# Layer two's input products taken in pairs of tiles, their low tail products on 64 rows each

## The chip, the core and the metric

One core of one Trainium2 chip runs the whole program. The time is device microseconds (us) of one execution. Engines are named as in the profile: PE (TensorE matmul), PEld (its weight loads), DVE (VectorE), ACT (ScalarE), POOL (GpSimd) and SP (SyncE, which issues the DMAs).

## What is computed

A softmax over seven weights per head and token makes a causal convolution of x, then two feed-forward layers follow, the first with a rational activation, the second with a clipped one. Everything is float32 in the reference.

```python
w = exp(weight_gen - max); w = w / (sum(w) + 1e-9)          # 7 weights per head
x = einsum("bshk,bskhg->bshg", w, unfolded_x)               # 8192 tokens x 192
h = x @ w_in                                                # 192 -> 2048
g = (a0 + a1*h + a2*h**2 + a3*h**3) / (1 + |b0|*|h| + |b1|*h**2 + 1e-6)
x = g @ w_out                                               # 2048 -> 192
h = x @ w_in2                                               # 192 -> 2048
out = (h * clip(h + 3, 0, 6) / 6) @ w_out2                  # 2048 -> 192
```

## The kernel before

The 8192 tokens go in 17 batches: two of 256 tokens and fifteen of 512. The 2048 inner features are 16 tiles of 128. A slice is one PSUM bank of 512 columns: one tile of a 512-token batch, or two tiles of a 256-token batch. That makes 256 slices for each layer.

Products of float32 accuracy are made of reduced-precision ones (float32r): each operand is cut into a high part and the low rest. The 192 input rows are a head of 128 and a tail of 64. For one tile, `mm_in` (L254) issues five products into the tile's bank: high weight by high x, high weight by low x and low weight by high x for the head; and for the tail two products with `wst`, whose upper 64 rows hold the high and whose lower 64 rows the low tail weights, while x's tail stands twice, in rows 0 to 63 and again in 64 to 127. So the first tail product gives high and low weights by high x together, and the second does the same with low x. `in1` (L282) calls `mm_in` for layer one, `in2` (L383) for layer two. `out1` (L362) makes five products of 512 columns for a tile of layer one's output, `out2` (L403) 32 products of 192 columns and full float32 for a quarter of layer two's output of 256 tokens.

Between `in1` and `out1` ACT, DVE and POOL make the rational function: seven operations on ACT, DVE and POOL's three (`pool_q`, `pool_m`, `pool_lo`, L308 to L357) among them. After `in2` come one Relu on ACT (`act_r2`, L388) and one operation on DVE (`dve_g2`, L395), which frees the bank. The convolution's multiplications (`conv_mul`, L158) run on POOL too, eight for a 512-token batch.

PSUM has six banks for this work: at most four slices of layer one (class h), and at most four of all else (class s: `in2`, transposes, `out2`, weight decoding). Weights come as pairs of 32-bit words and are decoded and cut by ACT, DVE and POOL in the first 150 us ("jobs": `in`, `pair` for the tail weights, `o1`, `o2`).

The order of all instructions is made before the program is written: `plan` (L746) is a list scheduler. It takes operations with a cost, a due time (in units of T) and their dependences, and appends to each engine what can start first, weighed by due time. Each engine then runs its list strictly in that order. The numbers NB to EV (L560 to L586) set due times and weights; the costs are written at `add`. They are the planner's figures, not times of the chip.

Of the kernel before, what the change touches and what calls it, by code (L numbers as in the profile page):

```python
# [19 lines left out]
def kernel(  # L20
# [230 lines left out]
            op=ALU.subtract,  # L251
        )

    def mm_in(i, xs, f, dst):  # L254
        xh, xl = xs
        w = win[i]
        fs = slice(f * P, (f + 1) * P)
        seq = [
            (w["hi"], xh[:, 0, :]),
            (w["hi"], xl[:, 0, :]),  # L260
            (w["lo"], xh[:, 0, :]),
            (wst[i], xh[:, 1, :]),
            (wst[i], xl[:, 1, :]),
        ]
        for n, (l, r) in enumerate(seq):
            nc.tensor.matmul(  # L266
                out=dst, lhsT=l[:, fs], rhs=r, start=(n == 0), stop=(n == len(seq) - 1),
                skip_group_check=True,
            )

    h1 = {}
    e1 = {}
# [108 lines left out]
    h2 = {}  # L381

    def in2(b, q):  # L383
        h = h2[b, q] = bank(("in2", b, q), [P, GW], "h2")
        for i in range(BF[b]):
            mm_in(1, xin[1, b], q * BF[b] + i, cols(b, h, i))
# [113 lines left out]
    def job_pair(i, c):  # L500
        src = (moe_w_in, moe2_w_in)[i]
        ss = [slice(k * CW * WS, (k + 1) * CW * WS) for k in (c, c + 1)]
        top, low = (wst[i][h * 64 : (h + 1) * 64, c * CW : (c + 2) * CW] for h in range(2))

        def cuts(w):
            a, z = w[0:64], w[64:P]
            return [
                cut(top[:, :CW], low[:, :CW], a),
                cut(low[:, CW:], low[:, CW:], z),
                (lambda: nc.scalar.activation(out=top[:, CW:], in_=z, func=AF.Copy), None),  # L510
            ]

        return dict(shape=[P, CW], src=[src[P:D, ss[0]], src[P:D, ss[1]]], cuts=cuts)
# [44 lines left out]
                    l(eng)  # L558

    NB = {"u": 2, "w": 3, "l": 2, "r0": 3, "ghi": 3, "glo": 2}  # L560
    T = 4.407
    X0P = -112.0
    LP = -8.378
    JP0 = 4.004
    JPT = 3.728
    JPU = 1.292
    PEN = 1.749
    CP = 5.419
    KP = 0.04
    WIN = 26.752  # L570
    SWL = 0.0
    BETA = 0.009
    C1 = -5.774
    CV = 5.626
    SM = 4.098
    XQ = -4.798
    XTP = 4.081
    XH = 2.095
    O1 = 4.281
    UM = 5.526  # L580
    I2 = -0.923
    SPR = 0.935
    R2 = 2.049
    O2 = 4.361
    OS = 0.653
    EV = 3.556  # L586
    ops = {}

    def op(key, eng, cost, prio, emit, after=(), take=(), lat=None):
# [41 lines left out]
    for u, (b, v) in enumerate(UB):  # L631
        t0 = S0[b] * T - (BV[b] - 1 - v) * 8 * T
        c = u // 2
        if u % 2 == 0:
            t = t0 - CV * T
            add("gen", "SP", 0.6, t - XQ * T if c else X0P, load_gen, c, lat=2.0,
                take=[("wg", 2, [("softmax_b", c)])])
            add("load", "SP", 5.3, t - XQ * T + 1.0 if c else X0P + 0.5, load_chunk, c, lat=2.0,
                take=[("x", 2, [("conv_mul", 2 * c + 1, 1, 1)])])
            add("softmax_a", "DVE", 1.7, t - SM * T, softmax_a, c, after=[("gen", c)])  # L640
            add("softmax_e", "ACT", 0.28, t - SM * T + 2.0, softmax_e, c, after=[("softmax_a", c)])
            add("softmax_b", "DVE", 2.7, t - SM * T + 4.0, softmax_b, c, after=[("softmax_e", c)],
                take=[("wk", 2, [("conv_mul", 2 * c + 1, 1, 1)])])
        for i in range(2):
            for z in range(2):
                t = t0 - CV * T + (2 * i + z) * T
                prev = [(u, i, 0)] if z else [(u, 0, 1)] if i else []
                flex = (("POOL", 1.25, 0.0), ("DVE", 0.85, CP))[: 1 + (u < 2)]
                add("conv_mul", flex, 0, t, lambda u, i, z, e="POOL": conv_mul(u, i, z, e), u, i, z,
                    after=[("load", c), ("softmax_b", c)] + [("conv_mul",) + k for k in prev],  # L650
                    take=[("prod", 2, [("conv_sum", u, i, z)])])
                add("conv_sum", "DVE", 0.78, t + 0.5 * T, conv_sum, u, i, z,
                    after=[("conv_mul", u, i, z)] + [("conv_sum",) + k for k in prev],
                    take=[("xc", 2, [("xT", u)])] if i + z == 0 else [])
        add("x_dup", "ACT", 0.2, t0 - XTP * T, x_dup, u, after=[("conv_sum", u, 1, 1)])
        add("xT", "PE", 0.44, t0 - XTP * T + 0.5, xT, u, after=[("x_dup", u)], lat=0.2,
            take=[("s", NS, [("x_lo", u)])])
        add("x_hi", "ACT", 0.5, t0 - XTP * T + 1.0 - XH, x_hi, u, after=[("xT", u)],
            take=[("xh0", 2, [("in1", S0[b] + SN[b] - 1)])] if v == 0 else [])
        add("x_lo", "DVE", 0.6, t0 - XTP * T + 1.6 - XH, x_lo, u, after=[("x_hi", u)])  # L660
    for b in range(len(BL)):
        n, last = BT[b], S0[b] + SN[b] - 1
        ca, cd = 0.066 + n / 1200, 0.075 + n / 960
        t = (last + O1 + 2) * T
        add("mid_y", "ACT", 0.22 + 2 * ca, t - UM * T, mid_y, b,
            after=[("out1", last)], take=[("ys", 1, [("mid_f", b)])])
        add("mid_f", "DVE", cd, t + 0.1 - UM * T, mid_f, b, after=[("mid_y", b)])
        add("mid_head", "ACT", ca, t + 0.2 - UM * T, mid_head, b, after=[("mid_y", b)],
            take=[("xh1", 1, [("in2", b, SN[b] - 1)])])
        add("mid_tail", "ACT", ca, t + 0.3 - UM * T, mid_tail, b,  # L670
            after=[("mid_f", b), ("mid_head", b)])
        add("head_lo", "DVE", cd, t + 0.4 - UM * T, head_lo, b, after=[("mid_head", b)])
        add("tail_lo", "DVE", cd, t + 0.5 - UM * T, tail_lo, b,
            after=[("mid_tail", b), ("head_lo", b)])
        cm = 5 * BF[b] * (0.0137 + n / 2400)
        tu = t + I2 * T
        for q in range(SN[b]):
            t2 = tu + q * T * SPR * BF[b] / 2
            f = (q + 1) * BF[b] - 1
            jobs_in = [done["in", 1, f // 4], done["pair", 1, f // 8 * 2]]  # L680
            add("in2", "PE", cm, t2, in2, b, q, lat=0.2,
                after=[("tail_lo", b), ("head_lo", b)] + jobs_in
                + ([("in2", b, q - 1)] if q else []),
                take=[("s", NS, [("dve_g2", b, q)])])
            add("act_r2", "ACT", 0.48, t2 + 1.0 - R2 * T, act_r2, b, q,
                after=[("in2", b, q)] + ([("act_r2", b, q - 1)] if q % 2 else []),
                take=[] if q % 2 else [("big", ST, [("out2", b, BV[b] - 1, (f + BF[b]) * 4 // NF)])])
# [58 lines left out]
    def plan():  # L746
# [26 lines left out]
        while len(seq) < len(ops):  # L773
            best = None
            banks = opens()
            any_open = min(banks)[0]
            class_open = {}
            for name, most in LIMIT.items():
                mine = sorted((t for t, n in banks if n == name), reverse=True)
                class_open[name] = max(any_open, mine[most - 1] if len(mine) >= most else 0.0)  # L780
            for e, rs in ready.items():
                pick = None
                while todo[e] and todo[e][-1]["key"] in end:
# [1 line left out]
                cur = todo[e][-1]["prio"] if todo[e] else 0.0  # L785
                for at, o, cost, pen in rs:
                    at = max(at, free[e])
                    for name, depth, _ in o["take"]:
                        if name in LIMIT:
                            at = max(at, class_open[name])  # L790
                            continue
                        ring = rings.get(name, [])
                        if len(ring) >= depth:
# [16 lines left out]
                run = run + cost if o["key"][0] in FULL else 0.0  # L810
            free[e] = at + cost
            end[o["key"]] = at + cost + (LAT[e] if o["lat"] is None else o["lat"])
            for name, depth, rel in o["take"]:
                if name in LIMIT:
                    i = min(range(NSB), key=lambda i: (banks[i][0], i))
                    slot[o["key"]] = i
                    held[i] = (name, rel)
                    continue
                rings.setdefault(name, []).append(rel)
# [42 lines left out]
```

## Time and profile before

| | us |
|---|---|
| median of three runs | 1333.9 (1333.36 to 1335.59) |
| the profiled execution, its own time | 1331.12 |
| its span, first to last instruction | 1329.3 |
| PE busy in the span | 1254.5 |
| POOL busy | 1174.8 |
| ACT busy | 1154.4 |
| DVE busy | 1104.0 |

The profiled execution lies 2.8 us under the median, and 1.8 us of it lie outside the span. The mean granted TensorE clock is 0.976 of full speed. A record of a matmul lasts longer than the distance to the next one, since matmuls overlap; what one costs in a dense row is the distance from start to start.

### The profile page before, as it was taken

The page shows a single profiled execution, that of the slowest core. Times are in us where ns is not written, and L with a number is a line of the kernel's source. Part 1 is how long each engine was busy: PE and PEld are TensorE (multiplying, and loading weights), DVE is VectorE, ACT ScalarE, POOL GpSimd, SP SyncE. Part 2 cuts the span into 40 slices and gives each one's busy share as a digit, 9 for nine tenths or more (in the row PEclk, how much of TensorE's full clock was granted, in tenths as well). Part 3 has the DMA queues.
Part 4 walks back from the last instruction along what each step waited for, and adds up shares of the span by engine and source line. Part 5 has one row for each costly group of instructions (what it writes and reads, how often), then busy time and mean ns, then how long its engine had stood idle before and what let it go on. Part 6 is the DMA issues. An engine that isn't in the chain of part 4 may idle for free.

```text
span 1329.3 us, 18514 instructions
## 1 busy us (share of the span) xinstructions
PE 1254.5 (94%) x6256; PEld 1097.1 (83%) x6256; DVE 1104.0 (83%) x1649; ACT 1154.4 (87%) x2064; POOL 1174.8 (88%) x934
## 2 busy tenths in 40 slices
PE   2567998999999999999999999999999999999998
PEld 2566996888988889898888989888888988888898
DVE  6888988989789897989789897898978898886841
ACT  5989998989899898989989898988989899898941
POOL 7999999999989999899988999889998999987830
PEclk9577998999999999999999999999999999999999
DMA  7323000100010100101010000100000000000000
GB/s 221 118 80 97 23 18 6 34 16 31 7 36 7 43 1 13 34 10 36 6 37 4 16 31 7 36 14 31 7 29 14 7 6 7 7 1 12 1 13 12
DMA packets 16119, 37.62 MB, mean 28 GB/s; under 512 B 1948, under 2 KB 12314, under 8 KB 16024
## 3 DMA queue, kind: packets, MB, share of 16 engines
q1 hardware_dynamic: 16024, 36.44, 8.5%
q8 instruction: 49, 0.80, 0.2%
q14 instruction: 46, 0.38, 0.1%
HBM read 30.14 MB, written 6.29 MB: 27 GB/s over the span
## 4 chain that ended last, share of the span: by engine, by line
PE 47%; ACT 21%; POOL 16%; DVE 9%; issue 6%; DMA 1%; SPq 0%; POOLq 0%; DVEq 0%; ACTq 0%
PE h L266 24%; PE y L410 12%; POOL w L346 5%; POOL w L309 5%; POOL glo L357 3%; ACT r L324 3%; ACT w L295 3%; ACT r L329 3%; ACT w L333 3%; ACT u L290 2%; ACT g L393 2%; PE y L374 2%; PE y L376 2%; PE y L378 2%; PE y L377 2%
## 5 line engine op out<-in xcount | busy, mean ns | idle before, releaser
L357 POOL TENSOR_TENSOR glo<-w,r 128x512 fp32r<-128x512 f32 x256 | 332.3, 1299 | 37.0 <-DVE w L350 19.5
L346 POOL TENSOR_TENSOR w<-w,ghi 128x512 f32<-128x512 f32 x256 | 331.9, 1299 | 27.8 <-DVE ghi L338 16.9
L309 POOL TENSOR_TENSOR w<-w,u 128x512 f32<-128x512 f32 x256 | 333.3, 1303 | 22.2 <-ACT w L295 13.4
L410 PE MATMUL y<-wo,g 128*128 128x192 f32 x2048 | 351.6, 326 | 0.0
L410 PEld LDWEIGHTS y<-wo,g 128*128 128x128 f32 x2048 | 338.3, 190 | 8.8
L295 ACT ACTIVATE w<-u,bab 128x512 f32<-128x512 f32 x256 | 209.8, 819 | 25.5 <-POOL glo L357 24.9
L338 DVE SCALAR_TENSOR_TENSOR ghi<-h,acol,r 128x512 fp32r<-128x512 f32 x256 | 190.6, 745 | 34.6 <-ACT r L329 29.2
L350 DVE SCALAR_TENSOR_TENSOR w<-h,acol,w 128x512 f32<-128x512 f32 x256 | 191.0, 746 | 32.6 <-POOL w L346 31.0
L266 PE MATMUL h<-xh,wst 128*128 128x512 f32 (+1 forms) x544 | 209.3, 385 | 1.8 <-POOL wst L488 1.8
L397 DVE SCALAR_TENSOR_TENSOR g<-g,h 128x512 f32<-128x512 f32 x256 | 174.7, 682 | 42.7 <-ACT g L393 41.9
L266 PE MATMUL h<-xl,wst 128*128 128x512 f32 (+1 forms) x544 | 208.9, 384 | 0.0
L302 ACT ACTIVATE l<-h,acol 128x512 f32<-128x512 f32 x256 | 200.7, 784 | 3.9 <-PE h L266 2.4
L313 DVE TENSOR_TENSOR l<-h,l 128x512 f32<-128x512 f32 x256 | 174.2, 685 | 35.7 <-ACT l L302 33.4
L324 ACT ACTIVATE r<-w 128x512 f32<-128x512 f32 x256 | 161.9, 632 | 44.3 <-POOL w L309 43.4
L164 POOL TENSOR_TENSOR prod<-x,wk 128x672 f32<-128x672 f32 x127 | 189.4, 1510 | 11.7 <-DMA x<-in_x_dram 4.5
L317 DVE SCALAR_TENSOR_TENSOR h<-l,acol,h 128x512 f32<-128x512 f32 x256 | 191.5, 751 | 7.4 <-ACT u L290 3.4
L393 ACT ACTIVATE g<-h 128x512 f32<-128x512 f32 x256 | 153.6, 600 | 18.2 <-PE h L266 17.9
L329 ACT ACTIVATE r<-r 128x512 f32<-128x512 f32 x256 | 161.2, 630 | 2.0
L290 ACT ACTIVATE u<-h 128x512 f32<-128x512 f32 x256 | 152.1, 594 | 9.9 <-PE h L266 9.7
L333 ACT ACTIVATE w<-w 128x512 f32<-128x512 f32 x256 | 160.2, 626 | 0.0
L266 PE MATMUL h<-xh,win0hi 128*128 128x512 f32 (+1 forms) x272 | 115.6, 425 | 15.8 <-DVE w L350 14.5
L266 PEld LDWEIGHTS h<-xh,wst 128*128 128x128 f32 x544 | 106.1, 195 | 21.6 <-POOL wst L488 2.1
(74 smaller groups left out, 2235.9 us busy)
## 6 DMA issues: line engine op xcount, KB each, us to landing
x<-in_x_dram SPq DMA_DIRECT2D x14, 960.0 KB, 4.6
st<-in_moe_w_out_dram SPq DMA_DIRECT2D x16, 384.0 KB, 3.2
out_dram<-osb SPq DMA_DIRECT2D x32, 192.0 KB, 1.9
st<-in_moe_w_in_dram SPq DMA_DIRECT2D x8, 512.0 KB, 5.8
st<-in_moe_w_in_dram SPq DMA_DIRECT2D x8, 256.0 KB, 6.1
wg<-in_weight_gen_dram SPq DMA_DIRECT2D x16, 112.0 KB, 2.0
x<-in_x_dram SPq DMA_DIRECT2D x1, 768.0 KB, 10.3
x<-in_x_dram SPq DMA_DIRECT2D x2, 216.0 KB, 4.6
```

The lines of the kernel that those rows point to most:

```text
L266: nc.tensor.matmul(out=dst, lhsT=l[:, fs], rhs=r, start=(n == 0), stop=(n == len(seq) - 1), skip_group_check=True,)
L295: nc.scalar.activation(out=w, in_=e1[sl]["u"], func=AF.Identity, scale=bab[:, 1:2], bias=bab[:, 0:1])
L302: nc.scalar.activation(out=l, in_=h1[sl], func=AF.Identity, scale=acol[:, 3:4], bias=acol[:, 2:3])
L309: nc.gpsimd.tensor_tensor(out=e["w"], in0=e["w"], in1=e["u"], op=ALU.mult)
L317: nc.vector.scalar_tensor_tensor(out=h, in0=e["l"], scalar=acol[:, 1:2], in1=h, op0=ALU.add, op1=ALU.mult)
L324: nc.scalar.activation(out=r, in_=e["w"], func=AF.Ln, bias=CEPS)
L329: nc.scalar.activation(out=r, in_=r, func=AF.Exp, scale=-1.0)
L333: nc.scalar.activation(out=w, in_=w, func=AF.Copy, bias=CEPS)
L346: nc.gpsimd.tensor_tensor(out=m, in0=m, in1=g1[sl][0].bitcast(F32), op=ALU.mult)
L350: nc.vector.scalar_tensor_tensor(out=m, in0=h1.pop(sl), scalar=acol[:, 0:1], in1=m, op0=ALU.add, op1=ALU.subtract)
L357: nc.gpsimd.tensor_tensor(out=glo, in0=e["m"], in1=e["r"], op=ALU.mult)
L410: nc.tensor.matmul(out=y2[b, v][:, s, :], lhsT=g2[b, q][:, c : c + P], rhs=wo2[:, n, :], start=(n == 0 and s == 0), stop=(n == NF - 1), sk ...
```

## The change

For the fifteen batches of 512 tokens, `in2` now handles two tiles at a time, q and q + 1. It takes two PSUM banks, issues the first four products of tile q and the first four of tile q + 1, and then one low tail product for each. The low tail product is no longer made on all 128 rows: `mm_low` multiplies 64 rows of `wst` by 64 rows of low x, rows 0 to 63 for an even tile and rows 64 to 127 for an odd one. The product of low weight and low x is dropped by this. So that an odd tile finds its high tail weights in the lower half, the two halves of layer two's `wst` are exchanged for odd tiles: `job_pair` now cuts them with four copies on ACT where there were three, and four subtractions on 64 x 256 elements where there were two on 64 x 512.

The planner counts the pair as one PE operation of 2.2 (before: two of 1.135), lets it take two banks at once, and has new numbers T to EV; the cost of `conv_mul` on POOL is 1.36 where it was 1.25. `SWL` is 14.0 where it was 0.0, which gives other work on PE a small penalty while a row of `out2` operations is shorter than 14 us.

```diff
+    def mm_low(i, xs, f, dst):
+        rows = slice(f % 2 * 64, f % 2 * 64 + 64)
+        nc.tensor.matmul(
+            out=dst, lhsT=wst[i][rows, f * P : (f + 1) * P], rhs=xs[1][rows, 1, :],
+            start=False, stop=True, skip_group_check=True,
+        )
...
-        for n, (l, r) in enumerate(seq):
+        for n, (l, r) in enumerate(seq[: 4 if half else 5]):
...
     def in2(b, q):
+        if BF[b] == 1:
+            for n in (q, q + 1):
+                h2[b, n] = bank(("in2", b, n), [P, GW], "h2")
+                mm_in(1, xin[1, b], n, h2[b, n], True)
+            for n in (q, q + 1):
+                mm_low(1, xin[1, b], n, h2[b, n])
+            return
...
+                (ha, da), (hz, dz) = cut(ta, None, a), cut(lz, None, z)
+                return [
+                    (ha, cut(ta[e], la[e], a[e])[1]),
+                    (hz, cut(lz[o], tz[o], z[o])[1]),
+                    (cut(la[o], None, a[o])[0], cut(ta[o], ta[o], a[o])[1]),
+                    (cut(tz[e], None, z[e])[0], cut(lz[e], lz[e], z[e])[1]),
+                ]
...
-    T = 4.407
+    T = 4.526
...
-    SWL = 0.0
+    SWL = 14.0
...
-                flex = (("POOL", 1.25, 0.0), ("DVE", 0.85, CP))[: 1 + (u < 2)]
+                flex = (("POOL", 1.36, 0.0), ("DVE", 0.85, CP))[: 1 + (u < 2)]
...
-        cm = 5 * BF[b] * (0.0137 + n / 2400)
+        two_f = BF[b] == 1
+        cm = 2.2 if two_f else 5 * BF[b] * (0.0137 + n / 2400)
...
+                    take=[("s", NS, [("dve_g2", b, k)], ("in2", b, k)) for k in qs])
```

On PE, in the middle of the program, before: one tile of layer two (`win1` and `wst_82` are layer two's weights, `xh` and `xl` the high and low x, `h` the bank) and behind it one of layer one (`win0`, `wst_81`).

```order
L266 MATMUL h_6800<-xh_6647,win1hi 128x512 [waits DVE_49]
L266 MATMUL h_6800<-xl_6648,win1hi 128x512
L266 MATMUL h_6800<-xh_6647,win1lo 128x512
L266 MATMUL h_6800<-xh_6647,wst_82 128x512
L266 MATMUL h_6800<-xl_6648,wst_82 128x512
L266 MATMUL h_6812<-xh_5953,win0hi 128x512 [waits DVE_49]
L266 MATMUL h_6812<-xl_5954,win0hi 128x512
L266 MATMUL h_6812<-xh_5953,win0lo 128x512
L266 MATMUL h_6812<-xh_5953,wst_81 128x512
L266 MATMUL h_6812<-xl_5954,wst_81 128x512
```

The same place on PE now, one pair of layer two's tiles:

```order
L266 MATMUL h_6805<-xh_6659,win1hi 128x512 [waits Activation_49]
L266 MATMUL h_6805<-xl_6660,win1hi 128x512
L266 MATMUL h_6805<-xh_6659,win1lo 128x512
L266 MATMUL h_6805<-xh_6659,wst_82 128x512
L266 MATMUL h_6810<-xh_6659,win1hi 128x512 [waits DVE_49]
L266 MATMUL h_6810<-xl_6660,win1hi 128x512
L266 MATMUL h_6810<-xh_6659,win1lo 128x512
L266 MATMUL h_6810<-xh_6659,wst_82 128x512
L273 MATMUL h_6805<-xl_6660,wst_82 128x512
L273 MATMUL h_6810<-xl_6660,wst_82 128x512
```

The number of matmuls is the same; the low tail product of the first tile moved behind the second tile's four products, the wait for the second bank stands in the middle of the pair, and the two rows of L273 are the products on 64 rows each.

On ACT, in the same part of the program, before: the two Relus (`g2<-h2`) that fill one pair of results, with operations of layer one (`l`, `u`) between them.

```order
L393 ACTIVATE g2_6213<-h2_6193 128x512
L302 ACTIVATE l_6217<-h1_6159,acol_74 128x512
L290 ACTIVATE u_6226<-h1_6207 128x512
L302 ACTIVATE l_6230<-h1_6207,acol_74 128x512
L393 ACTIVATE g2_6213<-h2_6219 128x512
```

Now:

```order
L407 ACTIVATE g2_6288<-h2_6257 128x512
L407 ACTIVATE g2_6288<-h2_6262 128x512
L297 ACTIVATE u_6299<-h1_6282 128x512
L309 ACTIVATE l_6302<-h1_6282,acol_74 128x512
L302 ACTIVATE w_6318<-u_6299,bab_76 128x512
```

Both Relus of a pair stand behind each other, since both banks are finished together.

On SP, at the start of the program, before: the loads of weights (`st`), of the convolution's weights (`wg`) and of x, in the order in which they are issued.

```order
L431 DMA st<-in_moe_w_in_dram 64x1024 x2
L431 DMA st<-in_moe_w_in_dram 128x1024 x3
L431 DMA st<-in_moe_w_in_dram 64x1024 x2
L431 DMA st<-in_moe_w_out_dram 128x2x384
L97 DMA wg<-in_weight_gen_dram 128x224
L118 DMA x<-in_x_dram 128x1536
```

Now:

```order
L445 DMA st<-in_moe_w_in_dram 64x1024 x2
L445 DMA st<-in_moe_w_in_dram 128x1024 x3
L97 DMA wg<-in_weight_gen_dram 128x224
L118 DMA x<-in_x_dram 128x1536
```

The second block of x moved ahead of the second pair of tail weights and the first output weights.

## Rows read from the trace of the kernel before

**Rows 1.** Page, part 1: busy us (share of the span) x instructions.

```profile
PE 1254.5 (94%) x6256; PEld 1097.1 (83%) x6256; DVE 1104.0 (83%) x1649; ACT 1154.4 (87%) x2064; POOL 1174.8 (88%) x934
```

**Rows 2.** Windows: length, busy us of each engine (x instructions), granted clock, DMA.

```profile
0.00:150.00 150.00, 90.33 (x500) 81.43 (x501) 126.28 (x198) 127.19 (x243) 132.59 (x117) 0.81 0.37 115
150.00:300.00 150.00, 144.95 (x727) 125.50 (x727) 132.85 (x204) 137.10 (x247) 143.59 (x114) 0.98 0.07 22
300.00:700.00 400.00, 397.00 (x1945) 344.74 (x1944) 346.88 (x516) 361.07 (x643) 375.87 (x296) 1.00 0.06 22
700.00:1300.00 600.00, 596.33 (x2940) 520.75 (x2939) 493.83 (x728) 525.00 (x929) 522.70 (x411) 1.00 0.04 13
1300.00:1330.00 30.00, 25.87 (x151) 24.71 (x149) 4.12 (x6) 4.01 (x8) 0.00 (x0) 1.00 0.04 14
```

**Rows 3.** Waits of PE, 150 to 1250 us: us in total, times, longest.

```profile
PE y L374 <- DVE xl L249: 9.4, 4, 4.6
PE y L377 <- POOL glo L357: 1.2, 1, 1.2
```

**Rows 4.** Chain in order of time: start us, us, what; three starts of layer two, one `out2` quarter.

```profile
990.05 3.41 PE h L266 x15
...
1041.10 2.60 PE y L410 x16
...
1066.33 3.45 PE h L266 x15
...
1142.62 3.42 PE h L266 x15
```

**Rows 5.** Timeline of PE, 699 to 712 us: start us, us, instruction.

```profile
700.75 0.39 PE L266 MATMUL h<-xh,win1hi 128*128 128x512 f32 x1
700.98 0.39 PE L266 MATMUL h<-xl,win1hi 128*128 128x512 f32 x1
...
711.85 0.39 PE L378 MATMUL y<-glo,wo1s 128*128 128x512 f32 x1
```

**Rows 6.** Timeline of PE around one `out2` quarter.

```profile
731.38 2.76 PE L410 MATMUL y<-wo,g 128*128 128x192 f32 x16
733.85 0.53 PE L266 MATMUL h<-xh,win0hi 128*128 128x512 f32 x1
734.21 0.40 PE L266 MATMUL h<-xl,win0hi 128*128 128x512 f32 x1
```

**Rows 7.** Timeline of POOL, 400 to 420 us.

```profile
413.97 1.48 POOL L164 TENSOR_TENSOR prod<-x,wk 128x672 f32<-128x672 f32 x1 [1.13 <-DVE wk L139]
415.30 1.28 POOL L346 TENSOR_TENSOR w<-w,ghi 128x512 f32<-128x512 f32 x1
416.55 1.27 POOL L309 TENSOR_TENSOR w<-w,u 128x512 f32<-128x512 f32 x1
```

**Rows 8.** Groups by line: busy us, mean ns of one, idle before.

```profile
L397 DVE SCALAR_TENSOR_TENSOR g<-g,h 128x512 f32<-128x512 f32 x256 | 174.7, 682 | 42.7 <-ACT g L393 41.9
L393 ACT ACTIVATE g<-h 128x512 f32<-128x512 f32 x256 | 153.6, 600 | 18.2 <-PE h L266 17.9
```

**Rows 9.** Groups by line and form: the cuts of weights on POOL.

```profile
L488 POOL TENSOR_TENSOR wst<-st,wst 64x512 fp32r<-64x512 f32 x8 | 10.4, 1305 | 0.6
L488 POOL TENSOR_TENSOR wo1l<-st,wo1h 128x256 fp32r<-128x256 f32 x7 | 5.3, 758 | 0.0
```

**Rows 10.** Chain in order of time, the first 50 us.

```profile
6.60 6.93 DMA st<-in_moe_w_in_dram
13.55 7.95 DMA x<-in_x_dram
...
44.57 1.32 POOL wst L488
48.17 2.47 PE h L266 x10
```

More of the change, by code (lines that the diff above doesn't have):

```diff
@@ L252, in tail_lo, with mm_in @@
         )
-    def mm_in(i, xs, f, dst):
+    def mm_in(i, xs, f, dst, half=False):
         xh, xl = xs
@@ L506, in cuts @@
             a, z = w[0:64], w[64:P]
+            if i == 1:
+                ta, la, tz, lz, a, z = (
+                    x.rearrange("p (f two c) -> p f two c", two=2, c=P)
+                    for x in (top[:, :CW], low[:, :CW], top[:, CW:], low[:, CW:], a, z)
+                )
+                e, o = (slice(None), slice(None), 0), (slice(None), slice(None), 1)
+                (ha, da), (hz, dz) = cut(ta, None, a), cut(lz, None, z)
[5 more added lines that the diff above has]
+                ]
             return [
@@ L560 @@
     NB = {"u": 2, "w": 3, "l": 2, "r0": 3, "ghi": 3, "glo": 2}
-    T = 4.407
+    T = 4.526
     X0P = -112.0
[L563 to L568, printed above, removed]
+    LP = -24.816
+    JP0 = 7.655
+    JPT = 3.582
+    JPU = 2.557
+    PEN = 1.47
+    CP = 2.718
     KP = 0.04
-    WIN = 26.752
-    SWL = 0.0
+    WIN = 34.243
+    SWL = 14.0
     BETA = 0.009
-    C1 = -5.774
-    CV = 5.626
-    SM = 4.098
+    C1 = -10.911
+    CV = 2.738
+    SM = 4.195
     XQ = -4.798
[L577 to L580, printed above, removed]
+    XTP = 6.208
+    XH = -1.81
+    O1 = 4.465
+    UM = 4.644
     I2 = -0.923
     SPR = 0.935
[L583 to L586, printed above, removed]
+    R2 = -0.879
+    O2 = 3.95
+    OS = 0.966
+    EV = 6.813
     ops = {}
@@ L668 @@
         add("mid_head", "ACT", ca, t + 0.2 - UM * T, mid_head, b, after=[("mid_y", b)],
-            take=[("xh1", 1, [("in2", b, SN[b] - 1)])])
+            take=[("xh1", 1, [("in2", b, SN[b] - 3 + BF[b])])])
         add("mid_tail", "ACT", ca, t + 0.3 - UM * T, mid_tail, b,
@@ L680 @@
             jobs_in = [done["in", 1, f // 4], done["pair", 1, f // 8 * 2]]
[L681 to L684, printed above, removed]
+            src = q // 2 * 2 if two_f else q
+            if src == q:
+                qs = (q, q + 1) if two_f else (q,)
+                add("in2", "PE", cm, t2, in2, b, q, lat=0.2,
+                    after=[("tail_lo", b), ("head_lo", b)] + jobs_in
+                    + ([("in2", b, q - len(qs))] if q else []),
+                    take=[("s", NS, [("dve_g2", b, k)], ("in2", b, k)) for k in qs])
             add("act_r2", "ACT", 0.48, t2 + 1.0 - R2 * T, act_r2, b, q,
-                after=[("in2", b, q)] + ([("act_r2", b, q - 1)] if q % 2 else []),
+                after=[("in2", b, src)] + ([("act_r2", b, q - 1)] if q % 2 else []),
                 take=[] if q % 2 else [("big", ST, [("out2", b, BV[b] - 1, (f + BF[b]) * 4 // NF)])])
@@ L775, in plan @@
             banks = opens()
-            any_open = min(banks)[0]
+            any_open, two_open = sorted(t for t, _ in banks)[:2]
             class_open = {}
@@ L779, in plan @@
                 mine = sorted((t for t, n in banks if n == name), reverse=True)
-                class_open[name] = max(any_open, mine[most - 1] if len(mine) >= most else 0.0)
+                for k, o_t in enumerate((any_open, two_open)):
+                    m = most - k
+                    class_open[name, k] = max(o_t, mine[m - 1] if len(mine) >= m else 0.0)
             for e, rs in ready.items():
@@ L787, in plan @@
                     at = max(at, free[e])
-                    for name, depth, _ in o["take"]:
+                    for name, depth, *_ in o["take"]:
                         if name in LIMIT:
-                            at = max(at, class_open[name])
+                            at = max(at, class_open[name, len(o["take"]) - 1])
                             continue
@@ L812, in plan @@
             end[o["key"]] = at + cost + (LAT[e] if o["lat"] is None else o["lat"])
-            for name, depth, rel in o["take"]:
+            for n, (name, depth, rel, *k) in enumerate(o["take"]):
                 if name in LIMIT:
-                    i = min(range(NSB), key=lambda i: (banks[i][0], i))
-                    slot[o["key"]] = i
+                    i = sorted(range(NSB), key=lambda i: (banks[i][0], i))[n]
+                    slot[k[0] if k else o["key"]] = i
                     held[i] = (name, rel)
```

## Prediction

> **What bounds the kernel now.** I began with the shares of the engines: PE 94%, POOL 88%, ACT 87% [rows 1]. An average over the span can hide a start that looks unlike the rest, so the windows come next [rows 2]. In the first 150 us PE is busy for 90.3 only, at a mean granted clock of 0.81, while POOL works 132.6, ACT 127.2 and DVE 126.3: weights are decoded there and the first slices filled, and PE waits for the others. From 150 us on PE is busy 144.95 of 150, 397.0 of 400, 596.3 of 600, at 0.98 to 1.00. So PE loses 59.7 us in the start, 5.05 + 3.0 + 3.67 = 11.7 in the next 1150, and about 3 behind its last product, where the last output goes out. The waits say the same: from 150 to 1250 PE's named waits sum to 10.6 us, one of them 4.6 long [rows 3]. In the chain, layer two's stretch begins at 990.05, 1066.33 and 1142.62 [rows 4]: 76.3 us for a batch of 512 tokens, with PE in nearly every piece. Hence a microsecond of PE work taken out of the steady part is a microsecond of the span, as long as no other engine is that near. POOL is the nearest: 375.9 of 400 from 300 to 700, which is 71.7 us in a batch of 76.3. From its own rows: a row of POOL's layer-one operations starts every 1.25 us, a convolution piece takes 1.33 [rows 7]; 48 of the one and 8 of the other make 70.6. ACT at 361.1 of 400 has 68.9.
>
> What does a product cost? Its record is 0.39 us long, but from 700.75 to 711.85 there are 49 steps, 0.2265 us each [rows 5]. This and not 0.39 is the price of one more or one less in a full row; the 0.163 between the two is the part of a record that lies under the next product.
>
> **The change part by part.**
>
> *Layer two's products.* There are 15 x 8 = 120 pairs. A pair was ten products, 2.265 us. Now it is eight full ones, 1.812, and two on 64 rows each. No row of this trace shows a product on 64 rows, so their price L is bounded. If the two run at the same time, one of them on the upper, the other on the lower half of the rows, and nothing is lost on the way in and out, L is one step, 0.2265, and the pair saves 0.2265: 27.2 us over 120 pairs. If they run one after the other with nothing lost, L is 0.453 and the pair costs what it did. To either comes the price of going from 128 rows to 64 and back. The nearest rows are changes of another kind: between float32r and full float32 products. A quarter of `out2` takes 2.60 [rows 4]; from its start at 731.38 to the second product behind it at 734.21 are 2.83 [rows 6], which is 2.60 + 0.2265: that change costs nothing. The other end is a product that may not begin under the one before: then the hidden 0.163 shows, once or twice in each pair. With the two halves together, L is 0.2265, 0.39 or 0.553 for none, one or two such tails, and the pair saves 0.2265, saves 0.063, or loses 0.10.
>
> I take the middle, one tail, because neither end has a row of the same kind: the change of format is free but leaves all 128 rows in use, and the hidden 0.163 is there in every record but shows nowhere. That is a choice and not a reading. It gives 120 x 0.063 = 7.6 us less on PE. All 120 pairs lie in the stretch where PE is the bound, since the two batches of 256 tokens, which fill the start, keep the old products. In a batch 76.3 becomes 75.8, or 74.5 with no tail at all; POOL's 71.7 stays under both.
>
> The Trainium skill has a rule that speaks against this change: in "TensorEngine Tiling (Array Packing)", section "Key Properties", it says that a change of the tiling mode drains the TensorE. No row here shows that change. With a drain of 0.163 at both ends of a pair the sum would be 12 us longer instead of 7.6 shorter; that is the rival of two tails below.
>
> *Banks and hands behind the pair.* A pair takes two banks of class s at once, and both come free after its end: two Relus of 0.60 and then the second result on DVE, 0.68 [rows 8], about 1.9 us, against 1.3 behind a single tile. The second tile's first product waits for DVE's release of its bank, and everything on PE queues behind it, `out1` and layer one's next slice with it, so ACT's and POOL's next inputs too. Between two pairs there stand, in most places, ten products of layer one (2.27 us) or ten and an `out2` quarter (4.9), so 1.9 us are over before the bank is asked for. I cost it at nothing; if that cover is gone the price is up to 0.68 for a pair.
>
> *Weight cuts.* Two jobs now have four subtractions on 64 x 256 where there were two on 64 x 512. At 1.305 for the old form and 0.758 for the nearest form with 256 columns [rows 9] that is 3.03 against 2.61, 0.8 us more on POOL in all, and two short copies more on ACT against two long ones less. POOL is busy 132.6 of the first 150 us, so at most these 0.8 reach the span. I take 0.5.
>
> *Loads.* The second block of x now goes ahead of the second pair of tail weights. It holds the queues from 13.55 for 7.95 us, and the tail weights follow that much later; but their cut on POOL, which releases PE at 48.17, stands at 44.57 [rows 10], about 20 us after that landing. Nothing.
>
> *The new plan.* The order changes everywhere. In the steady part it has the same shape: eight rounds in which layer two's tiles alternate with one layer-one slice, then the `out2` quarters with layer-one slices between. `out2` stands in 120 separate rows instead of 116, and by rows 6 such a change is free. In the start the instructions ahead of slice 16's last POOL operation are 112 instead of 111, on ACT 200 instead of 211, on DVE 175 instead of 179. At ACT's 0.52 us (127.2 us, 243 instructions) the eleven would be 5.7 us of ACT, but POOL, which is busier, has none less. I take 0 for the start, with bounds of 6 us to either side, and the steady waits, 11.7 us, as they are.
>
> *Sum.* 1331.1 - 7.6 + 0.5 = 1324.0 for an execution like the profiled one. This one was 2.8 us under the median of 1333.9, so the forecast in the median's terms is 1326.8.
>
> **The rivals.**
>
> *Nothing is lost (no tail).* 27.2 us less: 1306.7. For it: the one change that the trace shows is free [rows 6]. Against it: POOL at 71.7 of 74.5 us would leave little, so some of the gain may come back as waits.
>
> *Two tails: slower.* Every pair waits for the full product before it and again for its halves: L is 0.553 and 120 x 0.10 = 12.0 us are added: 1346. It decides from 0.113 us for each change on, where two of them eat the step that was saved. For it: 0.163 of every product lies hidden, and none of the changes in the trace is one of height.
>
> *The halves don't overlap.* Then the change doesn't do what it says: ten products as before, and with no tail the time stays: 1334. With tails it would be over 1350; I give that little.
>
> *The pair's banks hold PE.* Two pairs stand near each other while an `out2` bank is open, about twice a batch, 30 times, and the last eight pairs follow each other at once. If each of the 38 waits a DVE operation longer, 0.68, it is 26 us and with the gain of 7.6 the time is 1352; half of that, which I think the most that can be, is 1339.
>
> **How the numbers follow.** One tail 0.45, no tail 0.17, two tails 0.18, no overlap 0.08, banks 0.12. A difference under 0.2%, 2.7 us, can't be told from none. Of the forecast's 0.45 about 0.04 falls within that, if the start is 6 us worse; with the no-overlap case, same is 0.12. Faster is 0.41 and the 0.17, with 0.02 of the bank case where the start is better: 0.60. Slower is the rest, 0.28. The range goes from the case without tails, 1307, to the one with two, 1346; outside lie long bank waits and halves in sequence with tails.
>
> **What would show it.** In the changed kernel's timeline the eight full products of a pair should still step by 0.2265, the two of L273 should start nearly together, and the distance from the first of them to the next full product, with what is lost before the first, is L plus nothing else: 0.39 by the forecast, 0.2265 and 0.553 by the rivals, 0.453 or more with starts one step apart if they don't overlap. The batch's distance in the chain should be 75.8. If PE's waits after 150 us are well over 11.7 us with DVE as the releaser in front of L266, the banks are at work. PE's busy time in the first 150 us should stay at 90. The prediction is wrong if L is over 0.45, or if the start moves by more than 6 us.

## The result and the profile after

The changed kernel takes 1351.7 us (median of 4 runs, 1350.2 to 1351.8), the kernel before 1334.7 (median of 4): a ratio of 1.012, 95% interval 1.010 to 1.013. It is 17 us slower, where 1326.8 was predicted and the range ended at 1346. The profiled execution took 1351.8, its span is 1349.8.

The page of the changed kernel, part 1 (busy us, share of the span, instructions), against [rows 1]:

```profile
PE 1279.1 (95%) x6256; PEld 1063.1 (79%) x6256; DVE 1100.4 (82%) x1652; ACT 1153.7 (85%) x2063; POOL 1180.2 (87%) x938
```

With as many instructions, PE is busy 24.6 us longer. The other engines have the work that they had (POOL 5 us more). The windows, against [rows 2]:

```profile
0.00:150.00 150.00, 88.95 (x492) 78.48 (x493) 128.84 (x203) 127.61 (x245) 132.62 (x121) 0.85 0.37 115
...
300.00:700.00 400.00, 400.00 (x1922) 328.69 (x1921) 341.10 (x511) 354.57 (x631) 370.50 (x289) 1.00 0.06 20
700.00:1300.00 600.00, 600.00 (x2887) 495.13 (x2887) 485.83 (x725) 524.16 (x928) 533.04 (x417) 1.00 0.04 15
```

The start is as it was (88.95 us of PE against 90.33). In the steady part PE has no gap left, but 1922 products where there were 1945 in the same 400 us: on the mean a product takes longer, and POOL (370.5 against 375.9) and ACT (354.6 against 361.1) have grown emptier. PE is held by itself and not by others: in part 4 of the page, the chain of work that ended last, it has 86% of the span. Its waits from 150 to 1250 us, against [rows 3], columns us in total, times, longest:

```profile
PE y L381 <- DVE xl L249: 5.1, 2, 4.8
PE y L384 <- POOL glo L364: 1.1, 1, 1.1
```

A fixed point in a batch is the last `out1` product of a tile. The two rows are PE's timeline in the changed kernel, at slices 63 and 191 (start us, us):

```profile
365.94 0.39 PE L385 MATMUL y<-glo,wo1s 128*128 128x512 f32 x1
...
991.01 0.39 PE L385 MATMUL y<-glo,wo1s 128*128 128x512 f32 x1
```

That is 625.1 us for eight batches, 78.1 each. The same two points of the kernel before:

```profile
363.55 0.39 PE L378 MATMUL y<-glo,wo1s 128*128 128x512 f32 x1
...
979.64 0.39 PE L378 MATMUL y<-glo,wo1s 128*128 128x512 f32 x1
```

616.1, or 77.0 a batch. (The 76.3 of [rows 4] was that of three neighbouring batches; the mean of eight is longer, which the prediction missed.) So some 1.1 us are lost in each of the batches, and behind the last `out1` product the span has 51.8 us left instead of 50.2.

Where they are lost, PE's timeline at a pair of the changed kernel shows:

```profile
703.54 0.39 PE L266 MATMUL h<-xh,win1lo 128*128 128x512 f32 x1
703.77 0.39 PE L266 MATMUL h<-xh,wst 128*128 128x512 f32 x1
704.09 0.50 PE L273 MATMUL h<-xl,wst 64*128 64x512 f32 x2
704.51 0.50 PE L381 MATMUL y<-ghi,wo1h 128*128 128x512 f32 x1
704.85 0.40 PE L382 MATMUL y<-ghi,wo1l 128*128 128x512 f32 x1
705.09 0.39 PE L383 MATMUL y<-ghi,wo1s 128*128 128x512 f32 x1
```

Full products step by 0.23 as in [rows 5], and the two half products stand in one row, since they start 3 ns apart: they do overlap. But the first of them starts 0.32 behind the product before, the next full one 0.42 behind them, and the one behind that 0.34. From the last full product (703.77) to the second one behind the couple (704.85) are 1.08 us; less two steps of 0.2265, L is 0.63. The median over 104 pairs is 0.634. Ten full products took 2.265, the pair now takes 1.812 + 0.634 = 2.446: 0.181 more, 21.7 us over 120 pairs.

### The profile page after: what moved, and what is told of

It is laid out like the page before. It is cut to its first block, busy times and chain, and to the rows that moved or that the text cites. A ratio compares the mean times of both kernels' runs of the same rounds, so it can differ in the third digit from the quotient of the medians.

```text
span 1349.8 us, 18485 instructions
## 1 busy us (share of the span) xinstructions
PE 1279.1 (95%) x6256; PEld 1063.1 (79%) x6256; DVE 1100.4 (82%) x1652; ACT 1153.7 (85%) x2063; POOL 1180.2 (87%) x938
## 4 chain that ended last, share of the span: by engine, by line
PE 86%; ACT 5%; POOL 4%; DVE 3%; issue 1%; DMA 0%; SPq 0%; POOLq 0%; ACTq 0%; DVEq 0%
PE h L266 37%; PE y L424 24%; PE y L381 5%; PE y L384 4%; PE y L383 4%; PE y L382 4%; PE y L385 4%; PE h L273 4%; POOL prod L164 1%; POOL glo L364 1%; ACT w L302 1%; POOL w L353 1%; POOL w L316 1%; ACT r L336 1%; ACT l L309 0%
## 5 line engine op out<-in xcount | busy, mean ns | idle before, releaser
L266 PE MATMUL h<-xh,wst 128*128 128x512 f32 (+1 forms) x544 | 209.0, 384 | 6.4 <-POOL wst L502 6.4
L309 ACT ACTIVATE l<-h,acol 128x512 f32<-128x512 f32 x256 | 199.7, 780 | 3.9 <-PE h L266 3.9
L331 ACT ACTIVATE r<-w 128x512 f32<-128x512 f32 x256 | 161.9, 632 | 41.5 <-POOL w L316 39.9
L411 DVE SCALAR_TENSOR_TENSOR g<-g,h 128x512 f32<-128x512 f32 x256 | 169.9, 682 | 33.4 <-ACT g L407 30.5
L407 ACT ACTIVATE g<-h 128x512 f32<-128x512 f32 x256 | 147.1, 596 | 46.3 <-PE h L273 42.4
L336 ACT ACTIVATE r<-r 128x512 f32<-128x512 f32 x256 | 161.2, 630 | 1.5
L340 ACT ACTIVATE w<-w 128x512 f32<-128x512 f32 x256 | 160.5, 627 | 0.0
L266 PE MATMUL h<-xh,win0hi 128*128 128x512 f32 (+1 forms) x272 | 120.8, 444 | 11.3 <-DVE w L357 3.5
L266 PEld LDWEIGHTS h<-xh,wst 128*128 128x128 f32 x544 | 105.5, 194 | 26.9 <-POOL wst L502 7.1
L381 PE MATMUL y<-ghi,wo1h 128*128 128x512 f32 (+1 forms) x272 | 117.0, 430 | 8.2 <-DVE xl L249 8.2
```

Source lines behind the costliest of these rows:

```text
L266: nc.tensor.matmul(out=dst, lhsT=l[:, fs], rhs=r, start=(n == 0), stop=(n == len(seq) - 1), skip_group_check=True,)
L309: nc.scalar.activation(out=l, in_=h1[sl], func=AF.Identity, scale=acol[:, 3:4], bias=acol[:, 2:3])
L381: mm(out=a, lhsT=wo1h[:, n, :], rhs=gh, start=st, stop=False, **kw)
```

## Experiments

**The height alone.** All of the change stays, its order too, but the low tail products run on all 128 rows again, as in the kernel before.

```diff
-        rows = slice(f % 2 * 64, f % 2 * 64 + 64)
+        rows = slice(0, P)
```

> The changed kernel with its new plan and its pairs, but each low tail product on all 128 rows again, so PE never changes height; the number and order of instructions are those of the changed kernel. Theory (each change between 128 and 64 rows costs PE about 0.20 us, two in a pair): the ten products of a pair step by 0.2265 again, a batch is 76.3, PE busy falls from 1279 to about 1255, and the time is 1326 to 1331, at or a little under the kernel before, since PE waited 4 us less in the new plan. Rival (the new order and the pair's two banks cost the time, not the height): the time stays at 1345 to 1352.

Measured: 1342.3 (median of 6, 1340.7 to 1343.3), between the two expectations, against 1334.9 for the kernel before, ratio 1.006 (1.005 to 1.008). So the heights cost 9.4 of the 17 us; the rest, 7.4 us, is there with ten full products in a pair. On the timeline of PE the ten step as ever:

```profile
703.58 0.39 PE L266 MATMUL h<-xh,wst 128*128 128x512 f32 x1
703.81 0.61 PE L273 MATMUL h<-xl,wst 128*128 128x512 f32 x2
704.26 0.39 PE L381 MATMUL y<-ghi,wo1h 128*128 128x512 f32 x1
```

703.58 to 704.26 is three steps of 0.2265, so L is 0.453. And PE waits again:

```profile
300.00:700.00 400.00, 397.17 (x1938) 343.02 (x1937) 343.57 (x515) 356.39 (x636) 371.66 (x291) 1.00 0.07 23
```

No engine is busy all the time there, PE has the work of before, and yet a batch takes 77.7 us.

**No low tail products at all** in layer two (their part of the result is left out): the bottom of what they can cost.

```diff
-            for n in (q, q + 1):
-                mm_low(1, xin[1, b], n, h2[b, n])
```

> The changed kernel without the 240 low tail products of the pairs (that part of layer two's input is left out), everything else in place. Theory of the two changes of height: the pair loses the 0.634 us that its two products cost now, 76 us in 120 pairs, and the time is 1275 if PE alone is the bound; up to 1295 if POOL, at 71 us a batch against PE's 72.7, holds it. Rival (order and banks): over 1320.

Measured: 1335.0, as by the rival (over 1320) and not the theory: no better than the kernel before, a batch at 77.7. This was the run that turned the theory over: 54 us of PE's work are out (240 x 0.2265), and of the full-height kernel's time only 7.3 us have gone. PE has the gaps now, as a window shows:

```profile
300.00:700.00 400.00, 385.81 (x1855) 325.31 (x1854) 343.73 (x515) 355.09 (x636) 371.35 (x291) 1.00 0.07 22
```

They have several causes. PE's waits from 300 to 1280 us:

```profile
PE h L266 <- DVE w L357: 12.0, 22, 0.9
PE y L381 <- DVE xl L249: 9.2, 12, 1.3
PE h L266 <- DVE g L409: 7.6, 11, 0.8
```

**The couple twice.** The same products added once more, in the same stretch of 64 rows (the low part counts double in the result).

```diff
-            for n in (q, q + 1):
+            for n in (q, q + 1, q, q + 1):
```

> The changed kernel with the two products on 64 rows issued twice, one couple behind the other, in the same stretch (the low part is added twice). Theory (the price is paid per change of height): one more couple is one more step, 0.2265 us, 27 us in all: 1379. Rival (the price belongs to the 64-row products themselves, their weights are never loaded ahead): 0.43 to 0.63 each, 1403 to 1428.

Measured: 1376.0. PE's timeline:

```profile
703.58 0.39 PE L266 MATMUL h<-xh,wst 128*128 128x512 f32 x1
703.90 0.73 PE L273 MATMUL h<-xl,wst 64*128 64x512 f32 x4
704.56 0.50 PE L266 MATMUL h<-xh,win0hi 128*128 128x512 f32 x1
704.90 0.39 PE L266 MATMUL h<-xl,win0hi 128*128 128x512 f32 x1
```

1.32 us where there were 1.08: a second couple costs 0.23, one step. So the first one's 0.634 is 0.23 for the work and 0.41 for getting to 64 rows and back. And 24.3 us more for 120 x 0.23 = 27.6 of PE's work: on this side, where PE has no gap left, nearly all of it reaches the end. The second couple starts 0.335 behind the first, so the two changes of height lie apart here. The medians of the starts are 0.318 and 0.335 around the way in, 0.323 and 0.338 around the way out; less two steps each, the way in costs 0.20 and the way out 0.21.

**Both on the same half.** The second low product uses the lower rows as well (wrong half of the tail for every other tile).

```diff
-        rows = slice(f % 2 * 64, f % 2 * 64 + 64)
+        rows = slice(0, 64)
```

> The changed kernel with both low products on rows 0 to 63 (an odd tile gets its low weights there, so its low tail part is another one). Theory (the halves overlap because they lie on different rows): now the second starts 0.2265 us behind the first, or up to 0.34 if its weights can't be loaded ahead on the same rows, 27 to 41 us in all: 1379 to 1393. Rival (halves overlap wherever they lie): 3 ns apart as now, and 1352.

Measured: 1377.1; in the trace the second starts 0.335 behind the first instead of 0.003.

```profile
705.41 0.39 PE L266 MATMUL h<-xh,wst 128*128 128x512 f32 x1
705.72 0.73 PE L273 MATMUL h<-xl,wst 64*128 64x512 f32 x2
706.38 0.50 PE L266 MATMUL h<-xh,win0hi 128*128 128x512 f32 x1
706.72 0.40 PE L266 MATMUL h<-xl,win0hi 128*128 128x512 f32 x1
```

1.31 instead of 1.08. (0.335 is also the distance between the two couples above and, within 0.003, that of the first two products behind the way out, so I put 0.11 of it down to the change of height and not to the half; the second product on the same half then costs one step more.) The overlap of the halves is real and worth one step, 0.23; the change does what it says.

**A quarter of the columns.** The low products on 128 of 512 columns (the rest of their part left out), which tells work from the price of the change of height.

```diff
-            out=dst, lhsT=wst[i][rows, f * P : (f + 1) * P], rhs=xs[1][rows, 1, :],
+            out=dst[:, :P], lhsT=wst[i][rows, f * P : (f + 1) * P], rhs=xs[1][rows, 1, :P],
```

> The changed kernel with its low tail products on 128 instead of 512 columns (the low tail part of the other 384 columns is left out). Theory (a change of height costs 0.09 before the first product of the new height and 0.11 in its step, whatever the product): from the last full product's start to the second one behind the pair 1.087 falls by 384 columns, 0.16, to 0.927. Rival (the 64-row products stream at less than full speed): by 0.32 or more. The time falls little, 1346 to 1349, since the order's other engines stand at 77.7 us a batch and PE at 78.1 now.

Measured: 1340.8, below the 1346 expected, a batch at 77.7.

```profile
702.87 0.39 PE L266 MATMUL h<-xh,wst 128*128 128x512 f32 x1
703.19 0.33 PE L273 MATMUL h<-xl,wst 64*128 64x128 f32 x2
703.44 0.50 PE L381 MATMUL y<-ghi,wo1h 128*128 128x512 f32 x1
703.78 0.39 PE L382 MATMUL y<-ghi,wo1l 128*128 128x512 f32 x1
```

The distances ahead of the couple (0.32) and behind the next product (0.34) stay, the one between falls from 0.42 to 0.25: three quarters of the columns are worth 0.17, three quarters of a step, and the price of the changes doesn't depend on the columns. The time falls by 10.9 for 20.9 us of PE's work, and stops at the same 77.7 as without any low product.

**The kernel before without the low products.** Its tail products of layer two are left out, four per tile instead of five; every engine's order stays otherwise.

```diff
+        seq = seq[:4] if i and xh.shape[2] == GW else seq
```

> The kernel before, its own order, without the 240 low tail products of layer two in the 512-token batches (that part of layer two's input is left out). PE's work is then 72.7 us a batch, so what the batch takes more is held by the other engines in this order. Theory (it is the new order that holds the other engines at 77.7 us a batch, as the same omission showed there): the old order lets them go at 74 to 75, and the time is 1305 to 1318. Rival (the other engines stand at 76 to 78 in either order, so no saving on PE could have been cashed): 76 to 77 a batch and 1322 to 1332, most of the gain in the last 50 us.

Measured: 1326.4 beside 1336.0 for the kernel before. Of 54 us of PE's work 9.6 come back by these two; by the spans of the two profiled executions (1329.3 and 1324.6) it is 4.7. A batch takes 77.3, as long as before; what is gained lies behind the last `out1` product (46.6 us instead of 50.2). PE is then as loose as in the run without low products above:

```profile
300.00:700.00 400.00, 387.32 (x1849) 325.33 (x1849) 346.59 (x512) 356.88 (x637) 373.16 (x293) 1.00 0.07 22
```

Its two largest waits from 300 to 1280 us are for DVE's second result and DVE's `xl`:

```profile
PE h L267 <- DVE g L398: 11.1, 23, 1.2
PE y L375 <- DVE xl L249: 4.9, 3, 1.8
```

**Less work for POOL, less for ACT.** From that kernel, once POOL's operation of L309 on half its columns, once ACT's of `act_q` (the other halves are left out).

```diff
-        nc.gpsimd.tensor_tensor(out=e["w"], in0=e["w"], in1=e["u"], op=ALU.mult)
+        h = GW // 2
+        nc.gpsimd.tensor_tensor(
+            out=e["w"][:, :h], in0=e["w"][:, :h], in1=e["u"][:, :h], op=ALU.mult
+        )
```

> The kernel before without layer two's low tail products in the 512-token batches, and with POOL's first operation of a slice (w times u) on half of its columns (both parts left out). POOL's work in a batch falls from 71.7 by about 16 x 0.6 = 9.6 us, PE's is 72.7. Theory (POOL is what held that order at 77.3 us a batch): the batch falls to 73 to 75, the time to 1270 to 1295. Rival (the way of a slice through all engines and banks holds it): the batch stays at 76 or more, 1310 to 1326.

```diff
+        w = w[:, : GW // 2]
```

> The same kernel before without layer two's low tail products in the 512-token batches, now with ACT's last operation of a slice (w plus a constant) on half of its columns instead (both parts left out); ACT's work in a batch falls by about 16 x 0.25 = 4 us, POOL's stays. Theory (POOL holds it): 76.5 to 77.3 us a batch, 1318 to 1326. Rival (ACT, or the way through ACT, holds it): 73 to 75, 1275 to 1300.

Measured: 1286.5 and 1312.1. Part 1 of the pages, of the kernel before without low products, of that with half of POOL's operation, and of that with half of ACT's:

```profile
PE 1226.4 (93%) x6016; PEld 1045.2 (79%) x6016; DVE 1106.5 (84%) x1649; ACT 1150.9 (87%) x2064; POOL 1173.5 (89%) x934
```

```profile
PE 1207.4 (94%) x6016; PEld 1048.6 (82%) x6016; DVE 1088.2 (85%) x1649; ACT 1144.0 (89%) x2064; POOL 1039.7 (81%) x934
```

```profile
PE 1220.2 (93%) x6016; PEld 1045.4 (80%) x6016; DVE 1106.6 (84%) x1649; ACT 1103.3 (84%) x2064; POOL 1173.4 (90%) x934
```

POOL's 133.8 us less give 39.9 of time, ACT's 47.6 less give 14.3: 0.30 us each for a microsecond of work, with a batch at 74.05 and 76.2. Neither is the bound alone, and each counts for more than PE's 0.09 to 0.18. So PE's idle time in that kernel was in large part time in which it waited for a slice on its way through POOL, ACT and DVE. Both runs start from the kernel without low products; what less work on POOL or ACT gives while PE has all of its products wasn't measured.

**Pairs or numbers.** The change brings the pairs and a new set of the planner's numbers. Without low products, the two apart: the changed kernel with the old numbers, and the kernel before with the new ones.

```diff
-    T = 4.526
+    T = 4.407
...
-                flex = (("POOL", 1.36, 0.0), ("DVE", 0.85, CP))[: 1 + (u < 2)]
+                flex = (("POOL", 1.25, 0.0), ("DVE", 0.85, CP))[: 1 + (u < 2)]
```

> The changed kernel without the pairs' low tail products (left out), its order planned from the numbers T to EV of the kernel before and conv_mul at 1.25 again. Theory A (the new numbers make the order's 77.7 us a batch): under 76. Theory B (taking tiles in pairs, with two banks at once and both Relus together, makes it): 77.5 or more. In us: A 1305 to 1325, B 1330 or more.

```diff
+        seq = seq[:4] if i and xh.shape[2] == GW else seq
...
-    T = 4.407
+    T = 4.526
...
-                flex = (("POOL", 1.25, 0.0), ("DVE", 0.85, CP))[: 1 + (u < 2)]
+                flex = (("POOL", 1.36, 0.0), ("DVE", 0.85, CP))[: 1 + (u < 2)]
```

> The kernel before, single tiles, planned from the changed kernel's numbers T to EV and conv_mul at 1.36, without the low tail products of layer two in the 512-token batches (left out). Theory A (new numbers): 77 us a batch or more. Theory B (pairs): under 76 a batch.

Without low products, one execution each (the time for a batch in brackets):

| | old numbers | new numbers |
|---|---|---|
| single tiles | 1326.4 (77.3) | 1321.8 (76.5) |
| pairs | 1329.0 (77.0) | 1335.0 (77.7) |

The new numbers are the better ones for single tiles and the worse ones for pairs. Executions of the kernel before differ by up to 7 us, so of these four only the largest differences, the 13 between pairs and single tiles with the new numbers above all, say something each.

**Single tiles with the new numbers,** the full kernel. This is the diff of the last run without the line on `seq`.

> The kernel before with single tiles and all its products, planned from the changed kernel's numbers T to EV and conv_mul at 1.36. Theory (the new numbers make a better order, the pairs a worse one): without its low tail products this order stood at 76.4 us a batch, so with them PE's 76.3 and the others are level, and the time is 1323 to 1329, under the kernel before. Rival (level engines hinder each other): 77 us a batch or more, 1330 to 1336.

Measured: 1330.9 (median of 12, 1327.2 to 1334.3) beside 1334.2, ratio 0.997 (0.996 to 0.998). It lies between the two expectations, and it is better than both kernels: by 0.3%, as the new numbers' only gain.

**Pairs, but one tile after the other.** In a pair's place in the order PE does all five full products of the first tile, then all of the second, so that the first tile's bank is done half a pair earlier. The other engines' orders stay.

```diff
-                mm_in(1, xin[1, b], n, h2[b, n], True)
-            for n in (q, q + 1):
-                mm_low(1, xin[1, b], n, h2[b, n])
+                mm_in(1, xin[1, b], n, h2[b, n])
```

> The changed kernel's order on all engines, its pairs still placed as one block with two banks, but inside a block all five full products of the first tile stand before those of the second, so the first bank is finished 1.1 us before the second. No change of height. Theory A (77.7 us a batch comes from the first tile being finished late): 76.4 to 77.0 and 1328 to 1334. Theory B (it comes from how the planner spaces blocks of two, in the order of every engine): 77.5 to 77.8 and 1338 to 1342, as with full height and the low products last.

Measured: 1340.5 (one execution), a batch at 77.7, against 1342.3 with full-height pairs. It isn't the late end of the first tile.

## Why the prediction was wrong

The 17 us, by medians of these runs: the new numbers 1334.2 to 1330.9, 3.3 less; the pairs 1330.9 to 1342.3, 11.4 more; the change of height 1342.3 to 1351.7, 9.4 more. The price of the pairs holds with the new numbers; with the old ones, without low products, they differ from single tiles by 2.6 us only, which is within the spread, and the full pairs were not run with the old numbers.

From the forecast of 1326.8 to 1351.7 are 24.9 us. 17.0 of them are the couple, which was to give 7.6 and costs 9.4; 7.4 are the order (pairs and numbers), taken at nothing; the kernel before stood 1.0 higher beside the full-height run than in the forecast, and the 0.5 for the weight cuts comes off, since the 7.4 hold them already. So L and the order made the time longer. That it could hardly have become shorter lies in a step before them.

**The step that failed first, under the whole sum: "a microsecond of PE work taken out of the steady part is a microsecond of the span, as long as no other engine is that near".** PE's 98 to 100% in [rows 2] were read as the bound, and POOL's 71.7 of 76.3 as room of 4.6 us a batch. But a slice goes from engine to engine in orders that are fixed, and POOL, 94% busy, has its gaps where its input isn't there yet, not where they could be used. Part 4 of the page of the kernel before, the chain over the whole span, had a sign of it:

```profile
PE 47%; ACT 21%; POOL 16%; DVE 9%; issue 6%; DMA 1%; SPq 0%; POOLq 0%; DVEq 0%; ACTq 0%
```

PE has less than half. The prediction read the chain between 990.05 and 1142.62, where it is PE's alone and a batch takes 76.3. (A chain of PE doesn't price a saving either: of single tiles with the new numbers PE has 82%, and without the low products they are about 9 us faster, for 54 us of work.)

With 54 us of PE's work out of the kernel before, 3.6 us a batch, the batch didn't get shorter at all. Had L been the 0.39 of the forecast, or even 0.2265, next to nothing of the 7.6 or 27.2 us would have come; with no low product at all the pairs stand at 1335.0. So the rival of 1306.7 was out of reach, though POOL's limit stood in its "against". The other way round there is no such cushion: PE's added work is paid, first in part (9.4 of 21.7 us), then nearly in full (24.3 of 27.6). One for one is too much there as well: with the measured L the prediction's sum would be 1333.9 + 21.7 + 0.5 = 1356.

The Trainium skill, "Perfetto Trace Analysis", section "Identifying the Most-Contended Engine", takes the engine with the highest busy share as the one to work on, and says that TensorE's headroom is to be judged by its MFU (the share of its peak rate) or its weight loads' share, not by its matmul share. By the weight loads, POOL (88%) and ACT (87%) stand ahead of PEld (83%) in [rows 1]. The runs agree on the order, 0.30 us for a microsecond of POOL against 0.09 to 0.18 for PE; they don't agree on a single engine, since ACT gives 0.30 as well.

**The term that was mis-sized is L: 0.634, not 0.39.** One tail was chosen as the middle, and the measured value lies outside the upper bound, 0.553, and beyond the 0.45 that the prediction named as the sign of being wrong. The rival of two tails had the mechanism, a loss at each of the two changes, with 0.163 for each; a change costs 0.20 (0.408 / 2). The bound had the wait too long, 0.163 for about 0.09, and lacked the weights, about 0.11, in the PEld rows of the changed kernel:

```profile
703.32 0.19 PEld L266 LDWEIGHTS h<-xh,win1lo 128*128 128x128 f32 x1
703.54 0.19 PEld L266 LDWEIGHTS h<-xh,wst 128*128 128x128 f32 x1
704.08 0.19 PEld L273 LDWEIGHTS h<-xl,wst 64*128 64x128 f32 x2 [0.35 <-issue]
704.51 0.19 PEld L381 LDWEIGHTS y<-ghi,wo1h 128*128 128x128 f32 x1 [0.24 <-issue]
704.62 0.19 PEld L382 LDWEIGHTS y<-ghi,wo1l 128*128 128x128 f32 x1
```

In an ordinary row a product's weights are loaded one step ahead (703.54, for the product that starts at 703.77). Those of the first product behind either change are loaded when that product starts (704.08 with 704.09, 704.51 with 704.51). I read the 0.20 as about 0.09 until the change may begin (0.319 less a step) and about 0.11 of weights that nothing covers (0.338 less a step). The sum is measured, and the doubled couple shows it for each of the two changes; that the 0.11 are the weights is read off these rows and not tested. The Trainium skill, "TensorEngine Tiling (Array Packing)", section "Key Properties", says that a change of the tiling mode drains the TensorE. The trace agrees in that each change costs a wait; the 0.09 of it are less than the 0.163 of a whole tail. The prediction's own threshold, 0.113 for each change, was the right test, and 0.20 is well beyond it.

**"I take 0 for the start ... and the steady waits, 11.7 us, as they are": half right.** The start stayed (88.95 us of PE's work in it). The steady part did not: with the heights undone, a batch takes 77.7 instead of 77.0, and pairs cost 11.4 us against single tiles with the same numbers. The order lists were read for their shape around layer two, and a difference of how far apart the two tiles' work stands on POOL, ACT and DVE has no row in them. That it comes with the pairs and their numbers is shown by the table and the run of single tiles; that it isn't the first tile's end is shown by the last run.

Where PE loses it stands in the traces, at the seam of two batches. The first `out1` product of a batch needs DVE's second `xl` of the batch before, which follows from that batch's last `out1` product over ACT's copy `ys` and four more operations. First the full-height pairs, then single tiles with the same numbers:

```profile
596.02 0.39 PE L385 MATMUL y<-glo,wo1s 128*128 128x512 f32 x1
597.20 1.20 ACT L217 ACTIVATE ys<-y 64x512 f32<-64x512 f32 x2
601.15 0.69 DVE L249 TENSOR_TENSOR xl<-y,xh 128x512 fp32r<-128x512 f32 x1
601.90 0.50 PE L381 MATMUL y<-ghi,wo1h 128*128 128x512 f32 x1 [0.61 <-DVE xl L249]
```

```profile
597.29 0.39 PE L378 MATMUL y<-glo,wo1s 128*128 128x512 f32 x1
597.71 1.20 ACT L217 ACTIVATE ys<-y 64x512 f32<-64x512 f32 x2
601.66 0.69 DVE L249 TENSOR_TENSOR xl<-y,xh 128x512 fp32r<-128x512 f32 x1
602.41 0.50 PE L374 MATMUL y<-ghi,wo1h 128*128 128x512 f32 x1
```

With single tiles ACT begins the copy 0.42 behind the product, with pairs 1.18, because two operations of layer one (L336 and L340, 596.04 to 597.18) still stand before it. PE's next `out1` product comes 5.88 instead of 5.12 behind the last. From 300 to 1280 us PE waits so ten times with pairs, 6.5 us in all, and once with single tiles, 0.3. The 0.76 between the two is the size of what a batch loses: 77.7 against 77.0 with single tiles (slices 63 and 191 at 365.85 and 981.49). It shows where the order's delay reaches PE, not why ACT comes so late in it: without any low product a batch of pairs takes 77.7 too, and PE waits at the same place. That stays open.

**Confirmed:** the halves overlap (3 ns apart); ten full products cost what they did; PE doesn't wait for banks in the changed kernel (6.2 us of waits in all from 150 to 1250, none of them in front of L266, so the bank rival falls); the weight cuts and the moved load leave PE's work in the first 150 us within 1.4 us; and steps of full products are unchanged, within 0.01 us.

## What to carry to other kernels

Before a saving on the busiest engine is priced at one for one, leave the work out altogether and look whether the time follows: here 54 us less gave 5 to 10, and a saving of at most 27 was worth next to nothing. Read the chain's shares over the whole span, not over one stretch. A detour of TensorE to half the rows and back cost 0.41 us in place of a saved 0.23, so it pays only where several such couples, at 0.23 each, stand in one stretch. And numbers that set an order should be tried on the old code too: they were this change's only gain.

## What the runs showed of the hardware

- A change between 128 and 64 rows costs TensorE 0.20 us each way (0.41 for both with 512 columns and nearly the same with 128), while a change between float32r and full float32 products cost nothing [rows 6].
- The first product behind such a change has its weights loaded at its own start; the product behind it starts 0.11 us later than a step. Within the stretch of 64 rows, four half products take only 0.23 more than two.
- Two products on opposite halves of the rows start 3 ns apart and take one step; on the same half they start 0.335 apart, 0.11 of it from the change of height, and the pair takes 0.23 more.
